# 256 columns of one weight row taken out of the stream, and short vectors loaded as rows

## The chip, the cores and the metric

The kernel runs on one core of a Trainium2 chip. The metric is device time in microseconds (us) of one execution. The core has a matrix engine (TensorE, PE in the profile), VectorE (DVE), ScalarE (ACT), GpSimd (POOL), and SyncE (SP), which here only issues DMAs. Data come from device memory (HBM) into on-chip memory of 128 partitions (SBUF) by 16 DMA engines; matmuls write into PSUM.

## The reference

One token of decoding: x has 1024 entries, and everything is float32. The output mixes an attention block a and a feed-forward block b with a scalar gate.

```python
g = _sigmoid((x * gate_w).sum(-1, keepdims=True))
a = softmax((x @ wq) k_cache^T * Dh**-0.5) v_cache @ wo   # 32 query heads, 4 kv heads, 65536 keys, Dh = 128
r = x @ w_r
b = x + sigmoid(r) * ((silu(x @ w_gate) * (x @ w_up)) @ w_down)   # 1024 -> 3584 -> 1024
out = g * a + (1 - g) * b
```

(With one token the router's choice picks that token. The lines for a and b are shortened here.) The caches are 2 x 4 x 65536 x 128 floats, 268 MB; with wq, wo (16.8 MB each) and the three feed-forward matrices (14.7 MB each) about 346 MB are read once, and each number read is used in few operations.

## The kernel before, in words

All large inputs are laid out on the host as one stream of units with 128 rows, one row for each SBUF partition. `heads` holds, for each of 4 kv heads, 9 loads of [128, 16384] floats (8.39 MB, 64 KB a row): wq and the first chunk of K, then K and V chunk by chunk, and at the end wo. `ffn` holds w_gate, w_up and w_down as 6 loads of [128, 14336] floats (7.3 MB, 56 KB a row); TAIL = 14336 is four rows k of w_gate, so the first of them is w_gate's k = 0 to 3. A 128-row index d = (partition, k) splits x's 1024 entries: k = 0..7 is the contraction step.

SyncE (L112 to L125) issues the 42 loads in order into three buffers `stream[0..2]`. From the fourth on, each load first waits for a mark that PE sets when it has read the buffer's former content (`LAST`, L44; "s0 0" for the fourth load). The last two tail loads are cut in pieces (`ENDS`, L34), the last three pieces 4, 3 and 1 KB a row, each with a semaphore of its own, so that PE can use each piece as it lands. Then SyncE waits for VectorE and stores the output (L126 to L130).

ScalarE at the start issues two small loads (L147 to L151): `vecs`, which is x, gate_w and w_r as [128, 3, 8] floats (96 bytes a row), into `xk`; and x as 4 rows of 1 KB into rows 0, 32, 64 and 96 of `x_row`, after VectorE's memset of `x_row`.

VectorE clears some tiles (L186 to L193), waits for `xk`, copies x into column 0 of each of eight 32-wide blocks of `xp` (L195), and forms the two dot products for the gate and the router (L196 to L198), for which PE waits (L287). It scales `x_row` by 1 - g (L207), after a wait for x, and prepares selection matrices from the identity that GpSimd makes.

PE's order of work is written out: the dot products, then in a loop over the 4 kv heads the q projection (L297, mark "q"), q's transposition (L304), eight K chunks (L313, marks s0 to s7), eight V chunks (L325) and wo (L342). The tail is w_gate (into `ps_f`) and w_up (into `ps_u`) at L369, one matmul of FN = 448 columns for each k, e and j, then w_down at L388. `tail` (L351) waits for a load before the first matmul that reads it. ScalarE copies scores out of PSUM and takes exponentials in `scores`; VectorE transposes them (L244) for the V matmuls. `fin` takes the final sum (L267).

The tiles `xk`, `fin`, `q_sb` and `lb` have SBUF space of their own (L86 to L88).

Of the kernel before, what the change touches and what calls it, by code (L numbers as in the profile page):

```python
# [8 lines left out]
P = 128  # L9
D = 1024  # L10
G = 4
HG = 8
DH = 128
SK = 65536
F = 3584
# [4 lines left out]
KB = D // P  # L20
NQ = D // 4
FB = F // P
FN = F // 8
# [4 lines left out]
PER = UNITS // 2  # L28
BUFS = 3

TAIL = 14336
# [3 lines left out]

PIECES = [(0, 192), (192, NQ)]


HEAD = ["q", "qt"] + [f"s{c}" for c in range(NCH)] + ["mx"] + [f"v{c}" for c in range(NCH)] + ["o", "w"]
MARKS = ["dot"] + [f"{m} {g}" for g in range(G) for m in HEAD]  # L40
# [6 lines left out]
ACTED = {m: i + 1 for i, m in enumerate(ACTS)}  # L47


def gated_mix_kernel(nc, x, vecs, heads, ffn, out):  # L50

# [16 lines left out]
    pe, act, dve, pool, sp = nc.tensor, nc.scalar, nc.vector, nc.gpsimd, nc.sync  # L70

    stream = [nc.alloc_sbuf_tensor(f"st{b}", [P, 2 * CH], F32, align_bytes=256)[:, :] for b in range(BUFS)]
    scores = nc.alloc_sbuf_tensor("s", [P, NCH, 512], F32)[:, :, :]
# [3 lines left out]
    hp = scores[:, 2:4, :].rearrange("p a n -> p (a n)")[:, : FB * 32]  # L77
    att_sb = scores[:, 4, :]
    zeros = scores[:, 5, :]
    o_sb = scores[:, 0, :].rearrange("p (s d) -> p s d", s=4)  # L80

    def sb(name, *shape):
        t = nc.alloc_sbuf_tensor(name, [P, *shape], F32)
        return t[tuple(slice(None) for _ in range(len(shape) + 1))]

    xk = sb("xk", 3, KB)  # L86
    x_row, fin, q_sb = sb("x_row", NQ), sb("fin", NQ), sb("q_sb", 2 * NQ)
    ident, ones, md, lb = sb("ident", P), sb("ones", P), sb("md", P), sb("lb", P)  # L88
    sel, sel8, nsel, sel4 = sb("sel", 32), sb("sel8", HG), sb("nsel", HG), sb("sel4", 4)
    half, halves = sb("half", 2), sb("halves", 2, 32)  # L90
    xp, qp, op = sb("xp", KB, 32), sb("qp", 4, 32), sb("op", HG, 32)
# [3 lines left out]
    gate = sig[:, 0:1]  # L95
# [5 lines left out]
    ps_s = [ps_u[:, i, :] for i in range(2)]  # L101
    acc, ps_m, att, y = psum("acc", 512), psum("ps_m", P), psum("att", 512), psum("y", NQ)

    names = ["done", "fed", "x1", "x2", "acted", "pooled", "marked", "d2p", "d2a", "d2s", "self"]
    names += [f"ld{b}" for b in range(BUFS)] + [f"end{i}" for i in range(sum(map(len, ENDS.values())))]
    sems = {n: nc.alloc_semaphore(n) for n in names}
    nums = sorted(s.num for s in sems.values())
# [4 lines left out]
    for i in range(G * PER + NTAIL):  # L112
        b = i % BUFS
        if i >= BUFS:
            g, l = divmod(i - BUFS, PER)
            sp.wait_ge(sems["marked"], MARK[f"{LAST[l]} {g}" if g < G else ["gate 0", "gate 1", "up 0"][l]])
        if i < G * PER:
            sp.dma_start(stream[b], heads[i]).then_inc(sems[f"ld{b}"], 16)
        elif i - G * PER not in ENDS:
            sp.dma_start(stream[b][:, :TAIL], ffn[i - G * PER]).then_inc(sems[f"ld{b}"], 16)  # L120
        else:
            cuts = ENDS[i - G * PER]
            for c0, c1 in zip([0] + cuts, cuts):
                sp.dma_start(stream[b][:, c0:c1], ffn[i - G * PER, :, c0:c1]).then_inc(sems[f"end{len(ends)}"], 16)  # L124
                ends.append((i, c0, c1))  # L125
# [11 lines left out]
        out=ident, in_=ident, compare_op=ALU.not_equal, fill=1.0, base=0, pattern=[[-1, P]], channel_multiplier=1  # L137
# [3 lines left out]
    acted = []  # L141

    def tell(ins, name):
        acted.append(name)
        return ins.then_inc(sems["acted"])

    act.dma_start(xk, vecs).then_inc(sems["x1"], 16)  # L147
    act.wait_ge(sems["d2a"], 1)
    act.dma_start(
        x_row[::32, :], x.rearrange("(j n) -> j n", j=4)  # L150
    ).then_inc(sems["x2"], 16)  # L151
    act.wait_ge(sems["marked"], MARK["dot"])
    tell(act.activation(sig, ps_m[:, :2], AF.Exp, scale=-1.0), "sig")
    for g in range(G):
# [4 lines left out]
        for c in range(NCH):  # L159
            t = scores[:, c, :]  # L160
# [10 lines left out]
    def then(ins):  # L171

        own[0] += 1
        ins.then_inc(sems["self"])
        dve.wait_ge(sems["self"], own[0])
# [14 lines left out]
    dve.memset(qp, 0.0)  # L190
    dve.memset(zeros, 0.0)
    dve.memset(halves, 0.0)
    then(dve.memset(op, 0.0))  # L193
    dve.wait_ge(sems["x1"], 16)
    dve.tensor_copy(xp[:, :, 0], xk[:, 0, :])  # L195
    dve.tensor_mul(dots[:, 0, :], xk[:, 0, :], xk[:, 1, :])  # L196
    then(dve.tensor_mul(dots[:, 1, :], xk[:, 0, :], xk[:, 2, :]))
    to_pe(dve.tensor_reduce(dsum, dots, AX.X, ALU.add))  # L198
# [4 lines left out]

    then(dve.tensor_scalar(rest[:, 0:1], gate, -1.0, 1.0, op0=ALU.mult, op1=ALU.add))
    then(dve.tensor_mul(rest[:, 1:2], rest[:, 0:1], sig[:, 1:2]))
    dve.wait_ge(sems["x2"], 16)
    dve.tensor_scalar_mul(x_row, x_row, rest[:, 0:1])  # L207

    dve.wait_ge(sems["pooled"], 2)
# [62 lines left out]
    def mark(ins, name):  # L272
        marks.append(name)
        ins.then_inc(sems["marked"])

    def take(name, n=1):
        pe.wait_ge(sems[name], n).then_inc(sems[name], -n)  # L277
# [14 lines left out]
    with pe.Fori(0, G):  # L292
        loaded(0)
        for k in range(KB):
            for f in range(2):
                j = 2 * (k % 2) + f
# [23 lines left out]
        for c in range(NCH):  # L320
            loaded(1 + NCH + c)
            take("d2p")
            for m in range(NM):
                j = m % 4
# [3 lines left out]
                    stop=(c == NCH - 1 and m >= NM - 4),  # L328
# [10 lines left out]
        for h in range(HG):  # L339
            for f in range(2):  # L340
                j = 2 * (h % 2) + f
# [9 lines left out]
    def tail(first, n):  # L351
        i, c = divmod(first, TAIL)
        assert c + n <= TAIL
        if i < min(ENDS):
            if c == 0:
                take(f"ld{(G * PER + i) % BUFS}", 16)
        else:
            for e, (i1, c0, _) in enumerate(ends):
                if (i1 - G * PER, c0) == (i, c):
                    pe.wait_ge(sems[f"end{e}"], 16)  # L360
        return stream[(G * PER + i) % BUFS][:, c : c + n]


    for i, part in enumerate(("gate", "up")):
        ps = (ps_f, ps_u)[i]
        for k in range(KB):
            for e in range(2):
                for j in range(4):
                    ins = pe.matmul(  # L369
                        ps[32 * j : 32 * j + 32, e, :FN], xp[:, k, :], tail((i * KB + k) * F + (2 * j + e) * FN, FN),  # L370
                        start=(k == 0), stop=(k == KB - 1),
                    )
            if k % 4 == 3:
                mark(ins, f"{part} {k // 4}")
            if (part, k) == ("gate", 3):
                take("d2p")
                for j in range(4):
                    ins = pe.matmul(
                        acc[32 * j : 32 * j + 32, :NQ], halves[:, j // 2, :],
                        att_sb[:, j % 2 * NQ : (j % 2 + 1) * NQ], start=True, stop=True,  # L380
                    )
                mark(ins, "att")
    take("d2p")
    for b in range(FB):
        for c0, c1 in PIECES if b == FB - 1 else [(0, NQ)]:
            n = c1 - c0
            for j in range(4):
                ins = pe.matmul(  # L388
                    y[32 * j : 32 * j + 32, c0:c1], hp[:, 32 * b : 32 * b + 32], tail(2 * KB * F + b * D + 4 * c0 + j * n, n),
                    start=(b == 0), stop=(b == FB - 1 and c1 == NQ),  # L390
# [34 lines left out]
```

## Time and profile before

| what | value |
|---|---|
| three runs without profile | 806.32, 806.5, 806.61 us |
| the profiled execution's own time | 806.34 us |
| its span (first to last instruction) | 804.6 us |
| granted TensorE clock, mean | 0.758 |
| bytes read from HBM | 346.05 MB |

A profile page lists the busy time of each engine, then the span in 40 slices with one digit for the busy tenths, then the DMA queues: q1 is SyncE's queue, q10 ScalarE's; each line gives packets, megabytes and the share of 16 engines' span. A packet is a row that a DMA moves, or a completion of four bytes that raises a semaphore. A table of stretches lists, for each stretch of the span, its length and for each engine the busy us (with the number of instructions), then the granted clock, the DMA engines' mean busy share and GB/s. A row of instructions ends with the idle time before them and what ended it. Line numbers are those of the kernel before.

### The profile page before, as it was taken

The numbers are of one execution on the slowest core, as the hardware profiler recorded it, in microseconds if no ns is written. First come the engines' busy times: TensorE is split into PE (matmuls) and PEld (weight loads), VectorE is DVE, ScalarE is ACT, GpSimd is POOL, SyncE is SP. The second block draws the span as 40 slices with busy tenths as digits, with TensorE's granted clock in tenths as the row PEclk, the third lists the DMA queues.
The fourth block names the chain that finished last, engine by engine and source line by source line (L and its number), as shares of the span: only waits on it lengthen the run. The fifth ranks groups of instructions, "written<-read, shape, count | busy, mean of one in ns | idle before, by whom it ended". The sixth has DMA issues, their size and how long they took to land. (4 is left out here: it accounts for less than half of the span.)

```text
span 804.6 us, 6262 instructions
## 1 busy us (share of the span) xinstructions
PE 408.4 (51%) x2890; PEld 125.9 (16%) x2890; DVE 74.5 (9%) x154; ACT 44.5 (6%) x99; POOL 0.7 (0%) x6
## 2 busy tenths in 40 slices
PE   0544454545644464535644454456445545474466
PEld 0211111111211121111111111112111111121122
DVE  0200010000000020000100110000000100000310
ACT  0000030000000020000000200000000300000000
POOL 0000000000000000000000000000000000000000
PEclk9987686677777786777877686777866866787768
DMA  9999999999999999999999999999999999999998
GB/s 414 421 418 463 418 424 457 420 428 450 424 430 450 424 430 446 427 430 446 427 430 446 427 430 446 427 431 443 427 433 443 424 437 443 421 439 431 433 418 337
DMA packets 7083, 346.22 MB, mean 430 GB/s; under 512 B 920, under 2 KB 1056, under 8 KB 1312
## 3 DMA queue, kind: packets, MB, share of 16 engines
q1 hardware_dynamic: 6920, 346.04, 99.4%
q8 instruction: 9, 0.15, 0.1%
q10 hardware_dynamic: 152, 0.02, 0.0%
q14 instruction: 2, 0.02, 0.0%
HBM read 346.05 MB, written 0.00 MB: 430 GB/s over the span
## 5 line engine op out<-in xcount | busy, mean ns | idle before, releaser
L325 PE MATMUL acc<-st,pt 128*32 128x512 f32 x1024 | 153.0, 760 | 148.6 <-PEq L277 148.6
L313 PE MATMUL ps_u<-st,qp 128*32 128x512 f32 x1024 | 151.2, 753 | 145.1 <-PEq L277 145.1
L325 PEld LDWEIGHTS acc<-st,pt 128*32 128x32 f32 x1024 | 42.7, 135 | 256.0 <-issue 256.0
L313 PEld LDWEIGHTS ps_u<-st,qp 128*32 128x32 f32 x1024 | 42.1, 134 | 250.9 <-issue 250.9
L157 ACT ACTIVATE s<-ps_u 128x512 f32<-128x512 f32 x32 | 19.1, 597 | 560.3 <-PE ps_u L313 560.3
L229 DVE TENSOR_REDUCE mx<-s 128x1 f32<-128x512 f32 x32 | 22.0, 686 | 278.1 <-ACT s L157 278.1
L244 DVE STREAM_TRANSPOSE pt<-s 128x512 f32<-128x512 f32 x32 | 22.7, 711 | 199.8 <-PE acc L325 196.2
L297 PE MATMUL ps_u<-st,xp 128*32 128x512 f32 x128 | 24.4, 932 | 21.0 <-PEq L277 21.0
L369 PE MATMUL ps_u<-st,xp 128*32 128x448 f32 x128 | 17.8, 728 | 16.2 <-PEq L277 16.2
L162 ACT ACTIVATE s<-s,nb 128x512 f32<-128x512 f32 x32 | 22.6, 708 | 10.4 <-DVE nb L239 10.4
L369 PE MATMUL ps_f<-st,xp 128*32 128x448 f32 x128 | 15.0, 628 | 13.3 <-PEq L277 13.3
L388 PE MATMUL y<-st,s 128*32 128x256 f32 (+2 forms) x232 | 17.6, 463 | 7.8 <-DMA st<-in_ffn 5.2
L342 PE MATMUL att<-st,op 128*32 128x512 f32 x128 | 16.0, 642 | 2.4 <-PEq L277 2.4
L288 PE MATMUL ps_m<-dsum,ones 128*128 128x2 f32 x2 | 0.6, 349 | 24.0 <-PEq L277 24.0
L297 PEld LDWEIGHTS ps_u<-st,xp 128*32 128x32 f32 x128 | 6.1, 163 | 39.4 <-issue 39.4
L388 PEld LDWEIGHTS y<-st,s 128*32 128x32 f32 x232 | 8.9, 133 | 17.2 <-DMA st<-in_ffn 8.0
L369 PEld LDWEIGHTS ps_u<-st,xp 128*32 128x32 f32 x128 | 5.5, 143 | 28.5 <-issue 28.5
L248 DVE COPY s<-acc 128x512 f32<-128x512 f32 x4 | 2.8, 692 | 75.0 <-PE acc L325 75.0
L369 PEld LDWEIGHTS ps_f<-st,xp 128*32 128x32 f32 x128 | 5.1, 124 | 23.0 <-issue 23.0
L219 DVE COPY q_sb<-ps_u 128x512 f32<-128x512 f32 x4 | 2.8, 691 | 54.4 <-PE ps_u L297 54.4
L165 ACT ACTIVATE s<-ps_f 128x896 f32<-128x896 f32 x1 | 0.9, 917 | 105.4 <-PE ps_f L369 105.4
L342 PEld LDWEIGHTS att<-st,op 128*32 128x32 f32 x128 | 4.7, 118 | 10.4 <-issue 10.4
(62 smaller groups left out, 58.7 us busy)
## 6 DMA issues: line engine op xcount, KB each, us to landing
st<-in_ffn SPq DMA_DIRECT2D x4, 7168.0 KB, 44.1
st<-in_ffn SPq DMA_DIRECT2D x2, 3072.0 KB, 36.8
st<-in_ffn SPq DMA_DIRECT2D x1, 4096.0 KB, 34.5
st<-in_ffn SPq DMA_DIRECT2D x1, 2048.0 KB, 36.6
st<-in_ffn SPq DMA_DIRECT2D x1, 1024.0 KB, 38.5
st<-in_heads SPq DMA_DIRECT2D x36, 47.9
st<-in_ffn SPq DMA_DIRECT2D x1, 512.0 KB, 39.3
st<-in_ffn SPq DMA_DIRECT2D x1, 384.0 KB, 39.8
```

Source lines behind the costliest of these rows:

```text
L157: tell(act.activation(scores[:, c, :], ps_s[c % 2], AF.Copy), f"s{c} {g}")
L162: act.activation(t, t, AF.Exp, bias=nb, scale=SCALE, accum_out=sums[:, c : c + 1]), f"e{c} {g}"
L219: to_pe(dve.tensor_copy(q_sb, ps_s[0]))
L229: ins = dve.tensor_reduce(mx[:, c : c + 1], scores[:, c, :], AX.X, ALU.max)
L244: to_pe(dve.transpose(pts[:, c % 2, :], scores[:, c, :]))
L248: to_pe(dve.tensor_copy(o_sb, acc.rearrange("p (s d) -> p s d", s=4)))
L297: ins = pe.matmul(ps_s[0][32 * j : 32 * j + 32, :], xp[:, k, :], unit(0)[:, k * D + f * 512 : k * D + (f + 1) * 512], start=(k < 2), stop= ...
L313: ins = pe.matmul(ps_s[c % 2][32 * j : 32 * j + 32, :], qp[:, s, :], unit(1 + c)[:, (4 * s + j) * 512 : (4 * s + j + 1) * 512], start=(s = ...
L325: ins = pe.matmul(acc[32 * j : 32 * j + 32, :], pts[:, c % 2, 32 * m : 32 * m + 32], unit(1 + NCH + c)[:, m * 512 : (m + 1) * 512], start= ...
L342: ins = pe.matmul(att[32 * j : 32 * j + 32, :], op[:, h, :], unit(UNITS - 1)[:, h * D + f * 512 : h * D + (f + 1) * 512], start=False, sto ...
L369: ins = pe.matmul(ps[32 * j : 32 * j + 32, e, :FN], xp[:, k, :], tail((i * KB + k) * F + (2 * j + e) * FN, FN), start=(k == 0), stop=(k == ...
L388: ins = pe.matmul(y[32 * j : 32 * j + 32, c0:c1], hp[:, 32 * b : 32 * b + 32], tail(2 * KB * F + b * D + 4 * c0 + j * n, n), start=(b == 0 ...
```

## The change

Three things are done at once.

1. *Side columns.* The last 256 columns of w_gate's row k = 3 (all 128 partitions, 128 KB) are left out of the first tail load, whose rows become 1 KB shorter. They come instead from an input `side` of [32, 4, 256] floats into a tile of 32 partitions, in eight DMAs of four partitions each, 4 KB a partition. SyncE issues one right after each of the loads 0, 3, 6, ... 21. The partitions of a DMA are 4 apart: m, m+4, m+8, m+12 for the first four DMAs, 16 more for the last four. PE waits for all eight after w_gate's k = 4 and adds four matmuls with a contraction of 32 and 256 columns; the matmul of k = 3 that had those columns is cut to 192.
2. *Vectors as rows.* x, gate_w and w_r come as three DMAs of 4 rows of 1 KB each into rows i, 32 + i, ... of `x_row`, after its memset, and x's 128 entries for the side matmuls as [32, 4] floats; all are waited for together. VectorE transposes `x_row` in blocks of 32 into `xt`, which is the new `xk`. The split of the 1024 entries over partitions changes to suit, and wq, w_gate and w_up are laid out anew on the host.
3. *Shared space.* `xt`, `fin`, `q_sb` and `lb` now lie in slots of `scores`.

```diff
-    xk = sb("xk", 3, KB)
-    x_row, fin, q_sb = sb("x_row", NQ), sb("fin", NQ), sb("q_sb", 2 * NQ)
-    ident, ones, md, lb = sb("ident", P), sb("ones", P), sb("md", P), sb("lb", P)
+    fin = scores[:, 7, :NQ]
+    q_sb, lb = scores[:, 1, :], scores[:, 2, :P]
+    xs_sb = sb("xs_sb", 4)[:32]
+    xt = scores[:, 6, :NQ]
+    xk = xt.rearrange("p (k q) -> p q k", q=32)
+    side_sb, xs = sb("side", 4, SIDE)[:32], sb("xs", 4, 32)[:32]
...
             sp.dma_start(stream[b], heads[i]).then_inc(sems[f"ld{b}"], 16)
+            if i % 3 == 0 and i // 3 < 8:
+                rows = slice(i // 12 * 16 + i // 3 % 4, i // 12 * 16 + i // 3 % 4 + 13, 4)
+                sp.dma_start(side_sb[rows], side[rows]).then_inc(sems["side"], 16)
         elif i - G * PER not in ENDS:
-            sp.dma_start(stream[b][:, :TAIL], ffn[i - G * PER]).then_inc(sems[f"ld{b}"], 16)
+            n = TAIL - SIDE * (i == G * PER)
+            sp.dma_start(stream[b][:, :n], ffn[i - G * PER, :, :n]).then_inc(sems[f"ld{b}"], 16)
...
-    act.dma_start(xk, vecs).then_inc(sems["x1"], 16)
     act.wait_ge(sems["d2a"], 1)
-    act.dma_start(
-        x_row[::32, :], x.rearrange("(j n) -> j n", j=4)
-    ).then_inc(sems["x2"], 16)
+    for i in range(3):
+        act.dma_start(x_row[i::32, :], vecs[i].rearrange("(j n) -> j n", j=4)).then_inc(sems["x"], 16)
+    act.dma_start(xs_sb, xside).then_inc(sems["x"], 16)
...
+    dve.memset(xs, 0.0)
     then(dve.memset(op, 0.0))
-    dve.wait_ge(sems["x1"], 16)
+    dve.wait_ge(sems["x"], 64)
+    then(dve.transpose(xt, x_row))
     dve.tensor_copy(xp[:, :, 0], xk[:, 0, :])
+    dve.tensor_copy(xs[:, :, 0], xs_sb)
...
-    dve.wait_ge(sems["x2"], 16)
     dve.tensor_scalar_mul(x_row, x_row, rest[:, 0:1])
...
+                    n = FN - SIDE * ((part, k, e, j) == ("gate", 3, 1, 3))
                     ins = pe.matmul(
-                        ps[32 * j : 32 * j + 32, e, :FN], xp[:, k, :], tail((i * KB + k) * F + (2 * j + e) * FN, FN),
+                        ps[32 * j : 32 * j + 32, e, :n], xp[:, k, :], tail((i * KB + k) * F + (2 * j + e) * FN, n),
                         start=(k == 0), stop=(k == KB - 1),
                     )
+            if (part, k) == ("gate", 4):
+                pe.wait_ge(sems["side"], 128)
+                for m in range(4):
+                    pe.matmul(
+                        ps[96:128, 1, FN - SIDE : FN], xs[:, m, :], side_sb[:, m, :], start=False, stop=False,
+                        tile_position=(0, 96),
+                    )
```

More of the change, by code (lines that the diff above doesn't have):

```diff
@@ L36 @@
 PIECES = [(0, 192), (192, NQ)]
+SIDE = 256
 HEAD = ["q", "qt"] + [f"s{c}" for c in range(NCH)] + ["mx"] + [f"v{c}" for c in range(NCH)] + ["o", "w"]
@@ L47, with gated_mix_kernel @@
 ACTED = {m: i + 1 for i, m in enumerate(ACTS)}
-def gated_mix_kernel(nc, x, vecs, heads, ffn, out):
+def gated_mix_kernel(nc, vecs, xside, side, heads, ffn, out):
     pe, act, dve, pool, sp = nc.tensor, nc.scalar, nc.vector, nc.gpsimd, nc.sync
@@ L84, in sb @@
         return t[tuple(slice(None) for _ in range(len(shape) + 1))]
-    xk = sb("xk", 3, KB)
-    x_row, fin, q_sb = sb("x_row", NQ), sb("fin", NQ), sb("q_sb", 2 * NQ)
-    ident, ones, md, lb = sb("ident", P), sb("ones", P), sb("md", P), sb("lb", P)
+    xs_sb = sb("xs_sb", 4)[:32]
+    xt = scores[:, 6, :NQ]
+    xk = xt.rearrange("p (k q) -> p q k", q=32)
+    side_sb, xs = sb("side", 4, SIDE)[:32], sb("xs", 4, 32)[:32]
+    x_row, ident, ones, md = sb("x_row", NQ), sb("ident", P), sb("ones", P), sb("md", P)
     sel, sel8, nsel, sel4 = sb("sel", 32), sb("sel8", HG), sb("nsel", HG), sb("sel4", 4)
@@ L102, in gated_mix_kernel @@
     acc, ps_m, att, y = psum("acc", 512), psum("ps_m", P), psum("att", 512), psum("y", NQ)
-    names = ["done", "fed", "x1", "x2", "acted", "pooled", "marked", "d2p", "d2a", "d2s", "self"]
+    names = ["done", "fed", "x", "acted", "pooled", "marked", "d2p", "d2a", "d2s", "self", "side"]
     names += [f"ld{b}" for b in range(BUFS)] + [f"end{i}" for i in range(sum(map(len, ENDS.values())))]
@@ L401 @@
     a = {n: np.asarray(t) for n, t in inputs.items()}
-    wq = a["A_wq"].reshape(P, KB, G, HG * DH).transpose(2, 0, 1, 3).reshape(G, P, -1)
+    wq = a["A_wq"].reshape(4, KB, 32, G, HG * DH).transpose(3, 0, 2, 1, 4).reshape(G, P, -1)
     wo = a["A_wo"].reshape(G, HG, P, D).transpose(0, 2, 1, 3).reshape(G, P, -1)
@@ L410 @@
     down[:, -1] = np.concatenate([last[:, :, c0:c1].reshape(P, -1) for c0, c1 in PIECES], axis=1)
-    ffn = np.concatenate([t.reshape(P, -1) for t in (a["B_w_gate"], a["B_w_up"], down)], axis=1)
+    gate_up = [a[n].reshape(4, KB, 32, F).transpose(0, 2, 1, 3) for n in ("B_w_gate", "B_w_up")]
+    ffn = np.concatenate([t.reshape(P, -1) for t in gate_up + [down]], axis=1)
     arrays = {
-        "x": a["A_x"].reshape(D),
-        "vecs": np.stack([a[n].reshape(P, KB) for n in ("A_x", "gate_w", "B_w_r")], axis=1),
+        "vecs": np.stack([a[n].reshape(D) for n in ("A_x", "gate_w", "B_w_r")]),
+        "xside": a["A_x"].reshape(4, KB, 32)[:, 3].T,
+        "side": gate_up[0][:, :, 3, F - SIDE :].transpose(1, 0, 2),
         "heads": heads.reshape(G * PER, P, 2 * CH),
```

## The prediction

> **What bounds the kernel now.** I read the page first, from its head to its queues. Its second part has the span in 40 slices, with the DMA row as the mean busy share of the 16 DMA engines.
>
> ```profile
> span 804.6 us, 6262 instructions
> PE 408.4 (51%) x2890; PEld 125.9 (16%) x2890; DVE 74.5 (9%) x154; ACT 44.5 (6%) x99; POOL 0.7 (0%) x6
> ...
> DMA  9999999999999999999999999999999999999998
> ...
> q1 hardware_dynamic: 6920, 346.04, 99.4%
> ...
> q10 hardware_dynamic: 152, 0.02, 0.0%
> ```
>
> The DMA engines are full in every slice but the last; the busiest compute engine is at 51%. SyncE's queue q1, the stream of caches and weights, holds 99.4% of the DMA engines' time. So the time is bytes over rate, plus a start and an end. The rate is read from a table of long stretches of the run (busy times, then granted clock, DMA share, GB/s):
>
> ```profile
> 62.00:120.00 58.00, 29.46 (x194) 8.03 (x194) 6.62 (x13) 8.73 (x21) 0.00 (x0) 0.75 1.00 433
> ...
> 290.00:540.00 250.00, 128.23 (x870) 37.98 (x862) 20.39 (x42) 10.52 (x24) 0.00 (x0) 0.75 1.00 435
> ```
>
> At 435 GB/s one of 16 engines moves 27.2 GB/s, or 1 KB in 0.038 us. Then the chain that ended last, in order of time (start, length, what):
>
> ```profile
> 751.10 8.90 PE ps_u L369 x64
> ...
> 761.81 39.80 DMA st<-in_ffn
> 801.61 0.04 issue
> 801.65 0.69 PE y L388 x16
> 802.34 0.03 issue
> 802.37 0.48 DVE fin L267
> ```
>
> The last piece of w_down lands after 39.8 us in the queue; only 0.69 us of matmuls, 0.48 us of VectorE and the store of the output follow. That PE stands ahead of it (751.10) is no bound: the last tail unit is 7 MB, 17 us at 435 GB/s, so it began to move near 784.6, 22 us after its last piece was issued at 761.8. Matmuls may be 22 us late there before the stream has a gap.
>
> What is left is how evenly the 16 engines end. Quarter-microsecond stretches at the end, same columns:
>
> ```profile
> 798.00:799.00 1.00, 1.00 (x24) 0.48 (x16) 0.00 (x0) 0.00 (x0) 0.00 (x0) 1.00 0.96 397
> ...
> 800.00:800.25 0.25, 0.25 (x12) 0.02 (x3) 0.00 (x0) 0.00 (x0) 0.00 (x0) 1.00 0.69 271
> 800.25:800.50 0.25, 0.25 (x8) 0.00 (x0) 0.00 (x0) 0.00 (x0) 0.00 (x0) 1.00 0.69 274
> 800.50:800.75 0.25, 0.03 (x5) 0.03 (x5) 0.00 (x0) 0.00 (x0) 0.00 (x0) 1.00 0.60 238
> 800.75:801.00 0.25, 0.25 (x8) 0.12 (x8) 0.00 (x0) 0.00 (x0) 0.00 (x0) 1.00 0.54 217
> 801.00:801.25 0.25, 0.25 (x8) 0.00 (x0) 0.00 (x0) 0.00 (x0) 0.00 (x0) 1.00 0.50 180
> 801.25:801.50 0.25, 0.11 (x4) 0.00 (x0) 0.00 (x0) 0.00 (x0) 0.00 (x0) 1.00 0.36 123
> 801.50:801.75 0.25, 0.10 (x4) 0.10 (x8) 0.00 (x0) 0.00 (x0) 0.00 (x0) 1.00 0.03 8
> ```
>
> 0.69 is 11 of 16: five engines are done by about 800.0 (the early group). From 0.60 to 0.50, three more end between 800.5 and 801.05 (the middle). The last eight end from 801.25 to 801.6 (the late group). The end waits for the latest of 16, so five engines have 1.6 us to spare, three 0.6 to 1.1 us, eight next to none. From 800.0 to 801.6 the mean idle share is 0.25 x (0.31 + 0.31 + 0.40 + 0.46 + 0.50 + 0.64) + 0.1 = 0.76 us: no change in the split of the bytes alone can bring more than that.
>
> **The change part by part.** *Which engines.* q1 has 48 loads of 128 rows and one store of 4 rows, 6148 rows; 6920 - 6148 = 772 = 48 x 16 + 4. So a 128-row DMA leaves 16 completions, a 4-row DMA 4. q10 agrees: 128 + 4 rows, and 152 - 132 = 16 + 4. A 4-row DMA therefore runs on four engines, and the kernel's rows per engine are 8 for a 128-row DMA. [...]
>
> *Bytes taken from the stream.* The first tail load loses 1 KB in each of 128 rows, 8 KB an engine: 8 x 0.038 = **-0.30 us on all 16 engines**.
>
> *Bytes added.* [...] At 27.2 GB/s a row takes 0.151 us. The nearest row is the stretch 798 to 799, in which rows of 3 to 8 KB with their completions ran at 397 GB/s: 4096 / 24.8 = 0.165 us. I take that: 8 x 0.165 = 1.32, so net **+1.02 us on four engines**; with 0.151 it is +0.91. What a 4-row DMA costs its ring beyond that the trace of before doesn't isolate: 0 from below; from above, 0.43 us, an issue of SyncE's in the chain (below).
>
> *The small loads.* q10 falls from 152 to 3 x (4 + 4) + 32 + 16 = 72 packets: per engine from 9 to 3, on the four from 10 to 9. At nothing from below and at the price of 1 KB (0.038) from above, that is 0 to -0.23 us on twelve engines. They carry 96 bytes, so I take 0 and keep -0.23 for the range.
>
> *The start.* Three 4-row loads and a 32-row load are issued by ScalarE after the memset of x_row; VectorE then waits for all four and adds a transpose, a copy and a memset before PE can begin. The rows of the timeline (start, length):
>
> ```profile
> 0.75 0.41 ACTq L147 DMA_DIRECT2D xk<-in_vecs  x1
> 1.19 1.07 ACTq L149 DMA_DIRECT2D x_row<-in_x  x1
> ...
> 23.38 0.17 DVE L195 COPY xp<-xk 128x8 f32<-128x8 f32 x1 [20.81 <-DMA xk<-in_vecs]
> ...
> 27.36 0.35 DVE L207 TENSOR_SCALAR x_row<-x_row,rest 128x256 f32<-128x256 f32 x1 [1.75 <-DMA x_row<-in_x]
> ...
> 37.71 0.33 SPq L118 DMA_DIRECT2D st<-in_heads  x1
> ```
>
> SyncE issued the fourth load at 37.71, when PE had finished s0. Three loads of 8.39 MB at 435 GB/s are 57.9 us of stream, from about 2 us on: the first gap would come near 60, 22 us later. Issuing now takes 3 x 1.07 + 0.41 = 3.6 us from 1.19 on. The vectors come at 23.4 again if each small packet waits for one 64 KB row, as xk's eight seem to have; if each DMA waits 4.0 us behind the one before, as x_row did behind xk (27.36 against 23.38), 23.4 + 12 = 35.4. The added VectorE work is under 1 us: a transpose of 128x512 is 0.711 us, a copy as at L195 0.17. So 13 us late at worst, and 22 hide it: **0**. Without that cover the whole delay would be lost. The memset and the removed wait for x2 vanish in the same cover.
>
> ```profile
> L244 DVE STREAM_TRANSPOSE pt<-s 128x512 f32<-128x512 f32 x32 | 22.7, 711 | 199.8 <-PE acc L325 196.2 <-ACT s L162 3.5
> L388 PE MATMUL y<-st,s 128*32 128x256 f32 x216 | 16.9, 476 | 7.5 <-DMA st<-in_ffn 4.9 <-PEq L277 2.5
> ```
>
> *The matmuls.* Four of 256 columns after gate's k = 4, eight passes at 0.476 us: 3.8 us, less some tenths for the one cut to 192 columns. gate 1 comes late by that, and so SyncE's wait; the 22 us found above hide it: **0**. PE waits for "side", but its last DMA follows load 21 of 42, far ahead.
>
> *SyncE's queue.* Each short DMA is issued right behind a big one. At 0.43 us (or 1.07, as ScalarE's 4-row one) the next wait begins that much later, behind which only loads stand that have two whole units, 38 us, queued ahead: **0**.
>
> ```profile
> 760.38 0.43 SPq L124
> ```
>
> *Vectors in scores' space.* q_sb, lb, xt and fin are written at the same points of VectorE's order as before and the slots are rewritten by ScalarE only after PE's marks, which it waits for already. No wait is added: **0**.
>
> **The sum.** Twelve engines end 0.30 us sooner, four 1.02 us later, and the latest decides. If the four are all early, the end is 801.6 - 0.30. If the latest of them is in the middle group, it is 1.02 less its lead of 0.6 to 1.1: -0.1 to +0.4. If one is in the late group, +0.7 to +1.0. The views don't say. The packet records behind them (starts and lengths, no engine) can be linked end to start from the load of x onwards; my linking puts two of the four in the early and two in the middle group, one of these near its end. It crosses many near ties, so it only serves to choose: lead 0.6, **+0.4 us**. The profiled execution took 806.34, 1.7 more than its span; 806.74. The median of the three runs is 0.16 higher, and I state the forecast against it: **806.9**.
>
> **The rivals.**
> *All four early:* no engine gets later than the late ones, and these lose 0.30, to 0.53 with the small packets: 806.0 to 806.2. For it: five such engines exist. Against: drawn at random, four would seldom all be among five of 16. Chance 0.2.
> *One of the four late:* +0.7 to +1.0, 807.2 to 807.5. For it: eight of 16 are late. Chance 0.2.
> *A 4-row DMA holds its rings (the other side):* on queue q1, between two big loads, each of the eight stops four engines for a fixed time h. From h = (1.6 + 0.6 - 1.02) / 8 = 0.15 us the kernel is slower by over 0.2% (1.6 us, about what a measurement can tell from no change). At 0.43 it is 0.4 + 3.4 = +3.8: 810.3. Against: the pieces at the end, rows of 1 to 8 KB one DMA after the other, still ran at 397 of 435 GB/s. Chance 0.07.
> [...]
> *The change does not do what it says:* the vectors come so late that the stream has a gap, or the start shifts by more than I see. The stream's first 5 us moved 302 GB/s, so at most 1.5 us are there to win. Chance 0.03 on each side.
>
> ```profile
> 0.00:5.00 5.00, 0.00 (x0) 0.00 (x0) 1.66 (x7) 1.28 (x1) 0.70 (x6) 1.00 0.81 302
> ```
>
> **How the numbers follow.** Forecast 0.47 (806.4 to 806.9, the -0.1 to +0.4), all early 0.2, one late 0.2, rings held 0.07, start 0.06. The range 805.9 to 807.7 takes the first three with 0.1 to 0.2 for the median's scatter (806.32 to 806.61) and leaves 0.13 out. Within 0.2% lie all of these; slower 0.07 + 0.03 = 0.1, faster 0.03, same 0.87.
>
> **What would show it.** q1 should have 6920 + 64 = 6984 packets at 346.04 MB, q10 72. The stretches of the last 2 us should show five to ten engines ending together sooner and one to four alone at the end, with shares of 0.06 to 0.25 for about half a microsecond. s0's load should be issued by 50 us. The prediction is wrong if the rate in the stretches from 62 to 500 falls below 433, if q1 shows a gap, or if the end is sooner by more than 0.53 us.

## The result, and the profile after

The changed kernel takes 813.62 us (median of 21 runs, 806.46 to 820.37) against 806.54 (median of 21, 806.27 to 807.91): ratio 1.007, 95% interval 1.0055 to 1.0086. The forecast was 806.9, so the kernel is some 7 us slower than forecast. The times spread as those before do not: three runs are at 806.5 to 806.8, one at 809.6, twelve at 812.0 to 814.0 and five at 818.4 to 820.4; the ratio leaves four of the highest out as disturbed, though the experiments show that what lengthens them is the change itself.

The page of the changed kernel (of the run at 813.57):

```profile
span 812.2 us, 6290 instructions
...
DMA  9999999999999999999999999999999999999997
GB/s 414 414 456 420 417 458 421 440 423 430 449 429 414 387 388 391 436 439 421 442 426 437 442 423 442 426 439 439 433 436 423 439 439 436 424 447 427 429 420 334
...
q1 hardware_dynamic: 6984, 346.04, 99.4%
...
q10 hardware_dynamic: 72, 0.01, 0.0%
```

The packets are the 6984 and 72 that were forecast, and the DMA engines are as full as before. But three slices of 20.3 us, the 14th to 16th, move 387 to 391 GB/s. In long stretches of the same profile (columns as before, GB/s last):

```profile
180.00:254.00 74.00, 41.53 (x270) 12.72 (x262) 5.58 (x13) 2.99 (x5) 0.00 (x0) 0.73 1.00 433
258.00:318.00 60.00, 29.17 (x190) 7.81 (x182) 6.67 (x13) 7.54 (x19) 0.00 (x0) 0.70 1.00 388
323.00:540.00 217.00, 107.76 (x748) 31.64 (x744) 17.18 (x36) 10.52 (x24) 0.00 (x0) 0.76 1.00 433
540.00:745.00 205.00, 103.51 (x736) 31.81 (x729) 16.97 (x36) 10.53 (x24) 0.00 (x0) 0.77 1.00 435
```

The rate is 433 to 435 except from 258 to 318, where it is 388 at a DMA share of 1.00: the engines always had work, and each packet took longer. The packet records behind the views (start and length of each packet, no engine) put the loss closer: rows of 64 KB take 2.42 us, and from 256 to 320 us 2.71. From 258 to 290 us all 190 of them are equal to 0.01 us, so all 16 engines are slower alike. The fifth short DMA's rows pass at 254.5 to 255.6, the sixth's at 319.6 to 320.8. 65 us at 388 in place of 435 GB/s lose 65 x (1 - 388/435) = 7.0 us, which is the whole difference.

Start and end are as before. The timeline of the start, and the end of the chain that ended last (start, length, what):

```profile
22.83 0.45 DVE L211 STREAM_TRANSPOSE s<-x_row 128x256 f32<-128x256 f32 x1 [20.13 <-DMA xs_sb<-in_xside]
...
24.05 0.55 PE L305 MATMUL ps_m<-dsum,ones 128*128 128x2 f32 x2 [24.05 <-PEq L294]
```
```profile
768.17 40.98 DMA st<-in_ffn
809.16 0.04 issue
809.20 0.70 PE y L413 x16
...
809.92 0.48 DVE s L284
```

The vectors come at 22.8 us instead of 23.4, PE begins at 24.05 as before, and the last piece waits 41 us in the queue: neither engine made the stream wait.

### The profile page after: what moved, and what is told of

The parts are those of the page before. It is cut to its first block, busy times and chain, and to the rows that moved or that the text cites. A ratio compares the mean times of both kernels' runs of the same rounds, so it can differ in the third digit from the quotient of the medians.

```text
span 812.2 us, 6290 instructions
## 1 busy us (share of the span) xinstructions
PE 400.4 (49%) x2898; PEld 122.6 (15%) x2898; DVE 75.1 (9%) x157; ACT 44.5 (5%) x99; POOL 0.7 (0%) x6
## 3 DMA queue, kind: packets, MB, share of 16 engines
q1 hardware_dynamic: 6984, 346.04, 99.4%
## 5 line engine op out<-in xcount | busy, mean ns | idle before, releaser
L330 PE MATMUL ps_u<-st,qp 128*32 128x512 f32 x1024 | 148.5, 742 | 158.0 <-PEq L294 158.0
L342 PE MATMUL acc<-st,pt 128*32 128x512 f32 x1024 | 149.5, 746 | 156.0 <-PEq L294 156.0
L314 PE MATMUL ps_u<-st,xp 128*32 128x512 f32 x128 | 20.1, 784 | 14.5 <-PEq L294 14.5
L387 PE MATMUL ps_u<-st,xp 128*32 128x448 f32 x128 | 15.4, 644 | 16.6 <-PEq L294 16.6
L359 PE MATMUL att<-st,op 128*32 128x512 f32 x128 | 20.9, 811 | 2.4 <-PEq L294 2.4
L387 PE MATMUL ps_f<-st,xp 128*32 128x448 f32 (+1 forms) x128 | 14.0, 585 | 12.4 <-PEq L294 12.4
L236 DVE COPY s<-ps_u 128x512 f32<-128x512 f32 x4 | 2.8, 692 | 50.1 <-PE ps_u L314 50.1
```

Of the source, the lines that this page charges most:

```text
L236: to_pe(dve.tensor_copy(q_sb, ps_s[0]))
L314: ins = pe.matmul(ps_s[0][32 * j : 32 * j + 32, :], xp[:, k, :], unit(0)[:, k * D + f * 512 : k * D + (f + 1) * 512], start=(k < 2), stop= ...
L330: ins = pe.matmul(ps_s[c % 2][32 * j : 32 * j + 32, :], qp[:, s, :], unit(1 + c)[:, (4 * s + j) * 512 : (4 * s + j + 1) * 512], start=(s = ...
L342: ins = pe.matmul(acc[32 * j : 32 * j + 32, :], pts[:, c % 2, 32 * m : 32 * m + 32], unit(1 + NCH + c)[:, m * 512 : (m + 1) * 512], start= ...
L359: ins = pe.matmul(att[32 * j : 32 * j + 32, :], op[:, h, :], unit(UNITS - 1)[:, h * D + f * 512 : h * D + (f + 1) * 512], start=False, sto ...
L387: ins = pe.matmul(ps[32 * j : 32 * j + 32, e, :n], xp[:, k, :], tail((i * KB + k) * F + (2 * j + e) * FN, n), start=(k == 0), stop=(k == K ...
```

## The experiments

Theory A: each short DMA moves four engines against the other twelve, and some of the positions that result are slow ones. Theory B: a slow spell of the memory that is not the kernel's. Theory C: engines that write partitions which other engines write in the stream; the expectations call such writes foreign. The records here name no engine, so which engine writes which partition was the author's assumption and is not shown; what the runs can show is which partitions cost time. The change's first four short DMAs go to partitions 0 to 15, the last four to 16 to 31, and the stretch above begins at the fifth.

**The changed kernel again (e1).** No edit.

> The changed kernel again, unedited. In its first profile the stream ran at 386 GB/s instead of 435 from about 256 to 321 us, 7.4 us lost, and that stretch began at the fifth short DMA (254.9 us) and ended at the sixth (320.0). Theory A (four engines are moved against the other twelve by each short DMA, and some of the relative positions that result are slow ones): times again between 806.4 and 820.4, mostly near 813.7, and a slow stretch, if the profile has one, begins and ends at short DMAs. Theory B (a slow spell of the memory that has nothing to do with the short DMAs): the spells begin and end anywhere, and rows_only shows them as well.

813.89 us (812.32 to 819.81, 5 runs). The profiled run (819.81) has one stretch under 430, again from the fifth short DMA to the sixth, and deeper:

```profile
258.00:318.00 60.00, 29.58 (x190) 7.96 (x182) 6.67 (x13) 7.54 (x19) 0.00 (x0) 0.70 1.00 355
330.00:380.00 50.00, 27.13 (x194) 8.18 (x186) 3.54 (x8) 0.00 (x0) 0.00 (x0) 0.76 1.00 435
```

So this run near 819 has not two stretches, but one at 355. That it sits at the same short DMA twice speaks against B. The seventh and eighth short DMAs, to partitions 16 to 31 too, start nothing in either profile (433 to 435 GB/s after them): a short DMA there can start a stretch, but need not.

**Rows alone (e2).** The side columns go back into the stream; the load of x's 128 entries and the four side matmuls go too.

```diff
-SIDE = 256
+SIDE = 0
-            if i % 3 == 0 and i // 3 < 8:
...
-                sp.dma_start(side_sb[rows], side[rows]).then_inc(sems["side"], 16)
...
```

> The three row vectors, the transposition and the shared space stay; the side columns go back into the stream and the eight short DMAs are gone. Theory A: 806.1 to 806.9 in every run, no stretch under 430 GB/s. If the new layout, the row loads or the moved tiles are the cause: 809 to 820 as after.

806.57 (806.21 to 807.24, 10 runs), ratio 0.9997 (0.9987 to 1.0006). The row loads, the new layout and the shared space cost nothing that shows, and B, which would show here too, falls.

**Other partitions (e3).** The last four short DMAs go 16 partitions further on, to 32 to 47, so that the times can tell whether it hangs on where the rows go; the side tile is cleared at the start and the matmuls contract over 64 partitions, of which 32 hold zero weights.

```diff
-                rows = slice(i // 12 * 16 + i // 3 % 4, i // 12 * 16 + i // 3 % 4 + 13, 4)
+                rows = slice(i // 12 * 32 + i // 3 % 4, i // 12 * 32 + i // 3 % 4 + 13, 4)
...
```

> [...] Theory A: as after, 806.4 to 820 and mostly near 813.7.

806.57 (806.38 to 806.83, 10 runs), ratio 0.9999 (0.9989 to 1.0008). The loss is gone, with rows of the same number and size at the same places in the queue:

```profile
180.00:252.00 72.00, 40.69 (x274) 12.47 (x266) 5.58 (x13) 2.98 (x5) 0.00 (x0) 0.76 1.00 433
258.00:318.00 60.00, 29.07 (x210) 8.64 (x206) 6.67 (x13) 7.54 (x19) 0.00 (x0) 0.79 1.00 435
400.00:540.00 140.00, 66.00 (x460) 19.48 (x456) 12.26 (x24) 9.33 (x22) 0.00 (x0) 0.76 1.00 435
```

Theory A falls: four rows of 4 KB pass at each of the eight places here too.

**Sixteen rows of 1 KB (e4).** Each short DMA has 16 rows. The author took this as one row for every engine, an estimate from the packet counts of q10 in the changed kernel: its 4-row loads leave four completions each, its 32-row load 16 (72 = 3 x (4 + 4) + 32 + 16).

```diff
-                rows = slice(i // 12 * 16 + i // 3 % 4, i // 12 * 16 + i // 3 % 4 + 13, 4)
-                sp.dma_start(side_sb[rows], side[rows]).then_inc(sems["side"], 16)
+                rows, m = slice(i // 12 * 16, i // 12 * 16 + 16), i // 3 % 4
+                sp.dma_start(side_sb[rows, m], side[rows, m]).then_inc(sems["side"], 16)
```

> As after, same eight places in the queue and the same 16 KB each, but each short DMA moves 16 partitions of 1 KB, so that all 16 engines get one row of 1 KB from each and none moves against the others. Theory A: 806.1 to 806.8 in every run, no slow stretch. If short DMAs as such hold the rings: 809 to 820 as after.

822.21 (813.83 to 864.41, 5 runs), against A, which had 806.1 to 806.8. In its profile (860.72) there are several stretches, and the last one goes on with no short DMA left in the queue:

```profile
120.00:180.00 60.00, 25.35 (x192) 7.35 (x192) 4.26 (x8) 0.00 (x0) 0.00 (x0) 0.74 0.99 393
180.00:252.00 72.00, 38.62 (x238) 11.95 (x242) 4.21 (x11) 1.79 (x3) 0.00 (x0) 0.70 1.01 403
258.00:318.00 60.00, 29.43 (x194) 8.48 (x194) 6.68 (x13) 7.54 (x19) 0.00 (x0) 0.74 1.01 431
...
540.00:740.00 200.00, 96.07 (x644) 27.87 (x636) 15.77 (x34) 10.52 (x24) 0.00 (x0) 0.71 1.00 388
```

By the packet records stretches begin as the second, third and fourth short DMAs pass (80, 139 and 202 us). These write partitions 0 to 15, from the same 64 KB of `side` that the first four short DMAs of the changed kernel load into the same partitions at no cost. So neither the partitions as such nor the rows read make the loss; what has changed is how the 16 KB are split, into sixteen rows in place of four. That it is other engines which write the partitions then was not shown.

**One short DMA (e5 to e8).** To separate start and duration, e5 takes e2 and adds one DMA after load 12, 16 KB that nothing reads; e6 has it on partitions 0 to 12, where the changed kernel's first short DMA went at no cost. `SHORT` holds, for each load that is followed by one, the first partition, the number of rows (4 partitions apart) and the floats of a row. The diff is against e2.

```diff
+SHORT = {12: (16, 4, 1024)}
...
+            if i in SHORT:
+                p0, m, n = SHORT[i]
+                rows = slice(p0, p0 + 4 * m - 3, 4)
+                sp.dma_start(side_sb[rows, :n], side[rows, :n]).then_inc(sems["side"], 16)
...
```

> Rows_only plus a single short DMA, 16 KB that nothing uses: four rows of 4 KB into partitions 16, 20, 24 and 28 after load 12. Theory C, in the form that the runs so far leave (a short DMA whose four engines write other engines' partitions can put all 16 engines into a slow state that stays until another one ends it): slow from 255 us on with nothing to end it before the tail's cut loads, up to 12.4% of some 490 us, 61 us: 806.6 in runs in which it does not start, up to 868 in those in which it does. Theory A (the moved engines): at most 0.2 us more than rows_only. If four of them must add up: 806.6 in every run.

> [...] Theory C: 806.4 to 807 in every run. If any four-row DMA at that place does it: as e5.

> e5's DMA after load 12 and e6's after load 15. If any disturbance of the phases ends the slow state: a slow stretch only from 255 to about 321 us, 806.6 to 814. If only a DMA that writes other engines' partitions ends it: as e5, up to 868.

> e5 with one row of 4 KB alone, partition 16, so one engine. If one engine that writes elsewhere is enough: as e5. If it takes several at once: 806.4 to 807.

e5: 893.93 us (877.88 to 906.7, 4 runs), more than the 868 allowed for, as is e7's highest run. e6, `{12: (0, 4, 1024)}`: 806.75 (806.2 to 807.34, 10 runs), ratio 1.0003 (0.9994 to 1.0013). e7, `{12: (16, 4, 1024), 15: (0, 4, 1024)}`: 855.42 (831.06 to 939.32, 4 runs). e8, `{12: (16, 1, 1024)}`: 806.53 (806.23 to 807.68, 10 runs), ratio 1.0002 (0.9992 to 1.0011). e5 and e6 differ in nothing but the partitions and, with them, the rows of `side` that are read:

```profile
180.00:252.00 72.00, 39.37 (x270) 11.96 (x262) 5.58 (x13) 2.99 (x5) 0.00 (x0) 0.78 1.01 436
258.00:318.00 60.00, 29.38 (x190) 7.84 (x182) 6.68 (x13) 7.54 (x19) 0.00 (x0) 0.73 1.01 381
...
540.00:740.00 200.00, 89.27 (x596) 25.98 (x596) 14.72 (x31) 10.52 (x24) 0.00 (x0) 0.72 1.00 377
```
```profile
258.00:318.00 60.00, 32.40 (x210) 8.92 (x206) 6.67 (x13) 7.54 (x19) 0.00 (x0) 0.73 1.01 436
...
540.00:740.00 200.00, 104.18 (x708) 30.97 (x712) 15.89 (x33) 10.53 (x24) 0.00 (x0) 0.72 1.00 433
```

(The first fence is e5, the second e6.) One DMA of 16 KB makes the stream run at 377 GB/s for some 540 us that follow, in a profile of 877.88 us. By the packet records the rows are back at their normal length at 793 us, 44 us before the first row of the tail's cut loads. e7 shows that a short DMA to partitions 0 to 12 does not end it: that one passes at 325 us, and the rate is still 355 after it.

```profile
258.00:318.00 60.00, 27.58 (x190) 7.53 (x182) 6.67 (x13) 7.54 (x19) 0.00 (x0) 0.76 1.00 354
330.00:380.00 50.00, 19.93 (x152) 5.48 (x144) 2.46 (x5) 0.00 (x0) 0.00 (x0) 0.72 1.01 355
400.00:540.00 140.00, 74.27 (x506) 21.38 (x502) 13.65 (x28) 10.53 (x24) 0.00 (x0) 0.75 1.00 434
```

In this run it ended at 389.8 us, just where the packet records have a 16 KB fetch of instructions on q8. e8 shows that one row of 4 KB is not enough (436 GB/s from 258 to 318).

**Where, how much, when, and how long the rows (e9 to e12).** Each is e5 with one edit: `{12: (64, 4, 1024)}`; `{12: (16, 4, 64)}`; `{0: (16, 4, 1024)}`; and every load of the stream cut into four DMAs.

```diff
-            sp.dma_start(stream[b], heads[i]).then_inc(sems[f"ld{b}"], 16)
+            for c in range(0, 2 * CH, CH // 2):
+                sp.dma_start(stream[b][:, c : c + CH // 2], heads[i, :, c : c + CH // 2]).then_inc(sems[f"ld{b}"], 16)
```

> [...] Theory C: a slow state from 255 us on, times well over 810 as in e5 (878 to 907). If partitions 16 to 31 are special in some other way: 806.4 to 807.

> e5 with rows of 256 bytes in place of 4 KB, partitions 16, 20, 24 and 28. If it is enough that a foreign write occurs: as e5. If two writers must meet at a partition group for some tenths of a microsecond: 806.4 to 807, since 256 bytes pass in 0.01 us.

> e5's DMA after load 0 in place of load 12. Theory C alone: slow from 24 us on, up to 12 to 15% of 720 us, 890 to 920. If the engines must already have drifted apart (at 22 us they start a row within 0.5 us of each other, at 254 us over 1.9 us): 806.4 to 807.

> e5, with each load of the stream cut into four DMAs whose rows are 16 KB (14 KB in the tail) in place of 64 KB. In e5 the slow state ended where the tail's rows become shorter. If the state lives on rows of 64 KB that all engines repeat in step: it dies within some rows, 806.5 to 812 with some microseconds for three times more completions. If row length does not matter: as e5, over 850.

e9: 874.81 (807.29 to 916.09, 4 runs), one of them with no loss. So it is not partitions 16 to 31 as such. That other engines write 64 to 76 in the stream, on which theory C's forecast rested, no run shows; what e9 shows is that rows there cost time. e10: 806.6 (806.21 to 807.47, 10 runs), ratio 1.0001 (0.9992 to 1.0011): rows of 256 bytes do nothing. e11: 820.0 (806.6 to 897.53, 10 runs, one of them with no loss), so that the engines need not have drifted apart first; in its profile the stream is slow from load 0 on and at full rate from the tenth slice:

```profile
GB/s 407 356 353 403 363 400 388 378 400 417 441 422 441 422 442 435 432 441 429 445 426 438 426 438 426 441 435 432 445 426 445 426 438 426 431 440 437 428 418 340
```

The packet records have rows 27% longer than normal, then 12% from 52.3 us and normal ones from 187.5 us on, each change at a 16 KB instruction fetch. e12: 828.21 (820.11 to 829.03, 4 runs): rows of 16 KB do not prevent it. The time lies between the two that were forecast, since the stretch ends at 350 us; why it is short is open. That e5's stretch ended where the rows become shorter, as the expectation has it, does not hold (see above).

```profile
180.00:252.00 72.00, 38.39 (x274) 12.00 (x269) 5.58 (x13) 2.99 (x5) 0.00 (x0) 0.78 1.01 432
258.00:318.00 60.00, 28.91 (x194) 8.07 (x190) 6.68 (x13) 7.54 (x19) 0.00 (x0) 0.77 1.01 354
...
400.00:540.00 140.00, 66.43 (x474) 18.75 (x465) 12.58 (x23) 10.53 (x24) 0.00 (x0) 0.76 1.01 431
```

**What it takes to start (e13 to e15).** `{12: (16, 2, 1024)}`, `{12: (16, 4, 256)}` (rows of 1 KB, as x's four in the kernel before), and e5's DMA issued by ScalarE:

```diff
+        if g == 1:
+            act.dma_start(side_sb[16:29:4], side[16:29:4]).then_inc(sems["side"], 16)
         act.wait_ge(sems["d2a"], g + 2)
```

> [...] One engine (e8) did nothing, four cost 70 to 100 us. If two are enough: over 830. If it takes more: 806.3 to 807.5.

> [...] If 1 KB is too short when four engines write: 806.3 to 807.5 as with 256 bytes. If not: over 812 in most runs, and it is the queue or the time that spares x's rows.

> e5's short DMA issued by ScalarE in the second group instead of by SyncE, so that its rows come between two rows of a load instead of between two loads. Foreign writes as such: over 830 as e5, from the time of that DMA on. If only SyncE's queue does it: 806.3 to 807.5.

e13: 806.73 (806.25 to 807.08, 10 runs), ratio 0.9998 (0.9989 to 1.0008). e14: 806.58 (806.32 to 807.45, 10 runs), ratio 0.9999 (0.999 to 1.0009). Two rows of 4 KB or four of 1 KB are not enough. e15: 885.48 (823.78 to 916.11, 4 runs): it does not take SyncE's queue. ScalarE's issue is at 281.70 us, its rows pass at 286.0 to 288.1 by the packet records, and the rate falls within the stretch that holds them:

```profile
281.70 0.61 ACTq L170 DMA_DIRECT2D side<-in_side  x1
```
```profile
180.00:252.00 72.00, 37.44 (x270) 11.72 (x262) 5.58 (x13) 2.98 (x5) 0.00 (x0) 0.78 1.01 436
258.00:318.00 60.00, 26.78 (x186) 7.55 (x178) 6.67 (x13) 7.54 (x19) 0.00 (x0) 0.76 1.01 402
330.00:380.00 50.00, 21.36 (x138) 6.51 (x138) 2.11 (x6) 0.00 (x0) 0.00 (x0) 0.69 1.01 370
```

**What is shown and what stays open.** Shown: the short DMAs make the loss (e2), one alone is enough (e5), and it hangs on where its rows go. Four rows of 4 KB to partitions 16 to 28 or 64 to 76 lengthened 28 of 30 runs (e5, e7, e9, e11, e12, e15); such rows to partitions 0 to 15 and 32 to 47 alone never did (e3, e6: 20 runs, 806.20 to 807.34). In the changed kernel's stretch all 16 engines are slower alike (190 rows at 2.71 us, equal to 0.01). That what counts is which engine writes a partition is the author's reading, from e4 above all, and was not shown, since no record names an engine. Open is what in the hardware keeps it up when the rows have long passed, which unit it is that limits the rate, why a short DMA to partitions 16 to 31 or 64 to 76 sometimes starts nothing, and why the depth differs from run to run (388 and 355 GB/s in two runs of one kernel).

What ends a stretch is argued from times alone and was not tried. In the packet records of the six profiles with one short DMA to partitions 16 to 28 or 64 to 76, the rows are back at their normal length within 2 us of a fetch of instructions: at 792.9 us in e5, 389.8 in e7, 850.3 in e9, 187.5 in e11, 349.6 in e12 (8 KB, on q14) and 801.4 in e15. But other fetches ended nothing, such as the one of 16 KB at 602.6 in e9 or those of 8 KB at 293 to 296 in e5, e7, e9 and e12; and in both profiles of the changed kernel the stretch ends as the sixth short DMA passes, with no fetch near.

## Why the prediction was wrong, point by point

- *The bound, the start, PE's slack, SyncE's queue, the shared space, the packet counts:* right. e2 has the row loads, the layout and the shared space, at 0.9997 of before; e3 has the side columns and their matmuls too, at 0.9999. PE begins at 24.05 us in the profiles before and after. One slip in the small loads moves nothing in the sum: four engines had 11 small packets before (152 = 12 x 9 + 4 x 11), not 10.
- *The bytes, -0.30 and +1.02 us, +0.4 in sum:* not refuted, and not measured closer. That the eight short DMAs give one and the same four engines eight rows each, which the +1.02 us takes for granted, no run shows; what the runs show in its place is the time of e3 and its end, below. The rows of 4 KB themselves took 0.156 to 0.171 us in the changed kernel's packet records, where 0.165 was taken. e3 has them without the slow stretch: 806.57 against 806.60 on its chip, 0.0 with an interval of some 0.8 us either way. Its end does look as forecast: most engines are done by 801.5 us, and shares of 0.06 to 0.15 follow for 0.7 us, one or two engines alone:

```profile
801.25:801.50 0.25, 0.17 (x4) 0.16 (x8) 0.00 (x0) 0.00 (x0) 0.00 (x0) 1.00 0.54 193
801.50:801.75 0.25, 0.25 (x8) 0.00 (x0) 0.00 (x0) 0.00 (x0) 0.00 (x0) 1.00 0.15 53
801.75:802.00 0.25, 0.21 (x4) 0.00 (x0) 0.00 (x0) 0.00 (x0) 0.00 (x0) 1.00 0.10 37
802.00:802.25 0.25, 0.00 (x0) 0.00 (x0) 0.00 (x0) 0.00 (x0) 0.00 (x0) 1.00 0.06 20
```

- *The step that failed:* "What a 4-row DMA costs its ring beyond that the trace of before doesn't isolate: 0 from below; from above, 0.43 us". I priced the eight short DMAs as rows, on the engines that carry them, by the end's rows. The cost is not that of four engines and none of the DMA's own time: it falls on all 16 engines for as long as the stretch lasts, 7.0 us in the profiled run where the sum had 0, and it hangs on a thing that the sum did not look at, which partitions the rows go to. The rows at the end, from which I argued, are all of 128-row DMAs, which write all partitions; they could not show it.
- *The rival "a 4-row DMA holds its rings"* had the right side and the wrong mechanism: its price h was to be paid eight times. The second, third and fourth, to partitions 0 to 15, cost nothing (62 to 254 us at 433 to 435 GB/s), nor did the seventh and eighth in the profiled run (433 from 323 to 540 us), and one alone can cost 70 to 100 us (e5).
- *The other load of 4 rows.* x's four rows in the kernel before, to partitions 0, 32, 64 and 96, looked like a precedent. At 1 KB a row they started nothing (806.27 to 807.91 in 21 runs), and four rows of 1 KB to partitions 16 to 28 after load 12 did not either (e14: 806.32 to 807.45).
- *The sign to watch for* was named: "the prediction is wrong if the rate in the stretches from 62 to 500 falls below 433". It fell to 388. The mark was tight, though: the kernel before has 432 from 180 to 290 us in its own trace.

## What to carry to other kernels

A small DMA beside a stream that fills all 16 engines is not priced by its bytes alone: 16 KB cost 71 to 100 us here (e5). Try its rows on other partitions: four of 4 KB cost nothing on 0 to 15 and 32 to 47 (e3, e6: 806.57 and 806.75 us), and much on 16 to 28 and 64 to 76 (e5, e9: 893.93 and 874.81). Short rows are no safe way round: four of 1 KB or 256 bytes cost nothing (e14, e10: 806.58 and 806.6), sixteen of 1 KB did (e4: 822.21). And read the GB/s row for a step down that stays: a DMA share of 1.00 with fewer GB/s was a longer packet here, not a missing one (2.71 in place of 2.42 us at 388 GB/s). A kernel whose runs suddenly spread by some per cent after such an edit should be looked at run by run, since one profile shows only one of the cases.

## What the runs showed of the hardware that was not expected

One DMA of 16 KB, whose rows pass within about 1 us (254.5 to 255.6 for the fifth in the changed kernel), left the stream at 377 GB/s in place of 435 for some 540 us (e5), at 354 for some 600 us in e9. The slowdown comes in several depths (388 GB/s in the changed kernel and e4, 377 in e5, 367 in e15, 354 or 355 in e1, e7, e9 and e12), is the same for all 16 engines where the rows were compared (the changed kernel's 190), and survives a change of load, of source and of row length from 64 KB to 56 KB (e9, to 850.3 us). To partitions 16 to 28, one or two rows of 4 KB, four of 1 KB and four of 256 bytes started nothing in ten runs each (e8, e13, e14, e10: 806.21 to 807.68); sixteen of 1 KB to partitions 0 to 15 did (e4).
